# Retention in 64-token chunks from the fifth block on, with its output product split around the next block's states and scores

## The chip, the cores and the metric

One core of a Trainium2 chip runs the kernel. The metric is the time of one execution in microseconds of device time, as the median of several runs. The engines are named as in the profile: PE (TensorE, matrix products; PEld is its weight load), DVE (VectorE), ACT (ScalarE), POOL (GpSimd) and SP (SyncE, which issues most of the transfers). Products go to PSUM; DVE and ACT read them from there.

## What is computed

Two stages follow each other. The first is retention, a causal attention without softmax whose weights decay with distance. The second is a feed-forward layer with the activation h·cos(h).

```python
batch, n_heads, seq, head_dim = (8, 8, 576, 64)
scores = scale * np.matmul(q, k.transpose(0, 1, 3, 2))
gamma = 1.0 - 2.0 ** (-5.0 - np.arange(H, dtype=np.float32))
rel = pos[:, None] - pos[None, :]
Dmat = np.where(rel >= 0, gamma[:, None, None] ** rel[None, :, :], 0.0)
attn_out = np.matmul(scores * Dmat, v)
# 4608 tokens; 8 heads of 64 side by side
x = attn_out.transpose(0, 2, 1, 3).reshape(B * S, H * D)
h = x @ w_in            # 512 -> 2048
out = (h * np.cos(h)) @ w_out   # 2048 -> 512
```

## The kernel before

**Retention in blocks and chunks.** The 4608 tokens are 18 blocks of 256 (`BK`). The decay is put into q and k beforehand (`scaled`, L156: every token's q and k are multiplied by a power of gamma of its position, on POOL for most blocks), so that retention becomes plain causal linear attention. A block is cut into two chunks of 128 tokens. For each chunk and head there are four kinds of matrix products: *scores* (tile `sc`, L282), keys of the chunk against its queries, which DVE multiplies by a 0/1 causal mask on the way to `ret` (L292); *states* (tile `st`, L319), the 64x64 matrix of keys times values of the chunk; DVE adds it to the running sum `s` (L347 copies where a sequence begins, L349 adds), and ACT rounds the sums to `sb` (L359); the chunk's *own output* (tile `ov`, L375), masked scores times values; and the *carried output* (L407), queries times the rounded sum of all chunks before, into the same PSUM tile. ACT then rounds `ov` into the feed-forward input `xT` (L430). Blocks 0 to 3 order their tokens in even/odd pairs (`pair`, `NP_B = 4`) and have products and code paths of their own. A sequence has 576 tokens, so with chunks of 128 some are `mixed`: a sequence ends and another begins in their middle. Those use `mask_cmix`, and `v_odd`, a copy of the values with the first half zero.

Products of 64 contraction rows by 64 output columns use a quarter of the PE array; in the trace four of them, on the four quarters, start within some 10 ns. The score and carried products are such quarters, 128 tokens wide. The state and own products of a 128-token chunk use all 128 contraction rows and half of the columns.

**Feed-forward in rounds.** The feed-forward layer works in nine rounds, n = 0 to 8, of 512 tokens (`W`), two blocks each. In a round, `mm1` (L435) makes h in eight pieces; each piece has a PSUM tile `h` in one of the banks "a", "b" and "m" (each 4 KB for a partition, in the order `abmabmab` for most rounds, so that the eighth piece is in "b"). ACT makes cos(h) as a sine (L457), and DVE multiplies h by it into `gT` (L460). After that comes the second product, by a seven-product scheme (`mm2_seven`, L582): products 1, 2, 6, 4, 7, 5 and 3, in that order, 16 products each, into the small banks "n" (1, 6 and 7 accumulate there, then 3) and "st" (2, 4 and 5, each over the one before). It needs sums of quarters of `gT`, the tiles `gs` (`g_sum`, L487), on DVE and, for one of them, on POOL. ACT copies finished products to `ot` (`copied`, L592), DVE adds others to them (L590), and SP stores the results.

**Who orders the work.** The program is scheduled by hand: each engine runs its instructions in the order in which the code issues them. Between two of the seven products the code calls a *unit* from the table `at`, which does a part of the retention of the blocks for the next round. In rounds 3 to 7 there are two visits in a round: `first_unit` before product 2 and `second_unit` before product 5. A visit issues the states of the next block (into bank "st"), the output of the block before it (bank "m"), and the scores of the next block (its two chunks into banks "a" and "b"). Rounds 1 and 2 have units of their own (`first_scores`, `next_scores`, `last_outputs`; `only_intro`, `mid_unit`, `end_unit`), as the lead of the retention over the feed-forward layer is built up there. DVE operations that need not come at once (the second mask, the adds) are kept in `pend` and issued by the next `flush()`. In a first visit the issue order on DVE is: state sums, the rest of the sums `gs` 5 and 6 (`late_sums`), first mask, the add that frees bank "st" for product 4, second mask. In a second visit it is: state sums, the add that frees bank "n" for product 3, the masks. A step of preparation (POOL scales q and k and rounds v of a later block, SP transposes by DMA and loads another block) hangs on the stores.

Of the kernel before, what the change touches and what calls it, by code (L numbers as in the profile page):

```python
# [8 lines left out]
F32 = mybir.dt.float32  # L9
# [8 lines left out]
def kernel(  # L18
# [34 lines left out]
    MIX = PERK // 2  # L53
    AHEAD = 3
# [28 lines left out]
    mask_c = consts.tile([P, P], F32)  # L83
    mask_cmix = consts.tile([P, P], F32)
# [4 lines left out]
    v_odd = consts.tile([P, H, D], BF16)  # L89
# [5 lines left out]
    class Chunk:  # L95


        def __init__(self, j, k):
            self.j, self.k = j, k
            self.pair = j < NP_B  # L100
            self.rows = slice(k * HP, k * HP + HP) if self.pair else slice(0, P)
            self.t0, self.c0, self.p0 = j * BK + k * P, k * P, k * HP
            first, end = self.t0 % S, (self.t0 + P - 1) % S
            self.mixed = end < first
            self.fresh = first == 0 or self.mixed
            self.carry = 0 if first == 0 else S - first if self.mixed else P
            self.ends = end == S - 1

    chunks = [[Chunk(j, k) for k in range(2)] for j in range(NB)]
# [64 lines left out]
    def round_v(j, runs=(nc.gpsimd.tensor_copy,) * 2):  # L174
# [4 lines left out]
        for c in chunks[j]:  # L179
            if c.mixed and c.pair:  # L180
                nc.scalar.copy(v_mix[HP // 2 : HP], vb[HP // 2 : HP])
                nc.scalar.copy(v_mix[HP:], vb[HP:])
            elif c.mixed:
                nc.gpsimd.tensor_copy(v_odd[HP:], f[HP:, c.k])
# [40 lines left out]
    def q_cols(c, he, hg, n=HP):  # L225

        return tiles["qkT", c.j][he * D : he * D + D, 0, :, hg, c.p0 : c.p0 + n]

    def scores(j, banks):
# [3 lines left out]
        pss = [  # L233
            psum.tile([P, HG, 2, P], F32, tag=t, name="sc")
            if isinstance(t, str)
            else [psum.tile([P, HG, P], F32, tag=u, name="sc") for u in t]
            for t in banks
        ]
        if cs[0].pair:
            order = [(c, y, he, hg) for hg in range(HG) for y in range(2) for he in range(2) for c in cs]  # L240
            mask = mask_mix if any(c.mixed for c in cs) else mask_p
            for c, y, he, hg in order:
# [4 lines left out]
                    rhs=q_cols(c, he, hg),  # L247
# [22 lines left out]
        else:  # L270
            ret = ret.rearrange("p a b r i -> p (a b r i)").rearrange(
                "p (k a b i) -> p k a b i", k=2, a=2, b=HG
            )
            pss = [
                ps.rearrange("p b r i -> p (b r i)").rearrange("p (a b i) -> p a b i", a=2, b=HG)
                for ps in pss
            ]
            for c in cs:
                for hg in range(HG):
                    for i0 in range(0, P, HP):  # L280
                        for he in range(2):
                            nc.tensor.matmul(  # L282
                                pss[c.k][i0 : i0 + HP, he, hg, :],
                                lhsT=kT[he * D : he * D + D, 1, c.k, hg, i0 : i0 + HP],
                                rhs=q_cols(c, he, hg),
                                start=True,
                                stop=True,
                            )

            def masked(k):  # L290
                mask = mask_cmix if cs[k].mixed else mask_c
                nc.vector.tensor_tensor(  # L292
                    out=ret[:, k].rearrange("p a b i -> p (a b) i"),
                    in0=pss[k].rearrange("p a b i -> p (a b) i"),
                    in1=mask.unsqueeze(1).to_broadcast([P, H, P]),
                    op=ALU.mult,
                )
# [4 lines left out]
    def sums_of(j, bank):  # L302
# [3 lines left out]
        ps = psum.tile([P, 2, HG, D], F32, tag=bank, name="st")  # L306
        begun = set()
        for c in need:
            if pair:
                vb = v_mix if any(c.mixed for c in need) else tiles["vb", j]  # L310
                rows = slice(0, P) if c.k == 1 and need[0].k == 0 else c.rows
                parts = [(y, vb[rows, y]) for y in range(2)]
            else:
                rows = c.rows
                parts = [(c.k, v_odd if c.mixed else tiles["vb", j][:, c.k])]
            for hg in range(HG):
                for y, vs in parts:
                    for he in range(2):
# [3 lines left out]
                            rhs=vs[:, head(he, hg), :],  # L322
                            start=he not in begun,
                            stop=y == parts[-1][0],
# [4 lines left out]
        def add():  # L329
            s32 = stp.tile([P, len(need), HG, D], F32, tag="s32", name="s32")  # L330
# [13 lines left out]
            else:  # L344
                for u, c in enumerate(need):
                    if c.fresh:
                        (nc.scalar.copy if j == 4 else nc.vector.tensor_copy)(s32[:, u], ps[:, c.k])  # L347
                    else:
                        nc.vector.tensor_tensor(  # L349
                            out=s32[:, u],  # L350
                            in0=ps[:, c.k],
# [5 lines left out]
            def rounded(run=nc.scalar.copy):  # L357
                sb = stp.tile([P, len(need), HG, D], BF16, tag="sb", name="sb")
                run(sb, s32)  # L359
# [7 lines left out]
    def out_own(j, ps):  # L367
# [4 lines left out]

        def one(c, h, y, rhs):
            part = (h % 2, h // HG)
            nc.tensor.matmul(  # L375
                ps[h % 2 * D : h % 2 * D + D, h // 2, c.c0 : c.c0 + P],
                lhsT=vb[c.rows, y, h, :],
                rhs=rhs,
                start=part not in begun,
                stop=False,  # L380
                skip_group_check=True,
            )
            begun.add(part)

        if chunks[j][0].pair:
            for swap in (1, 0):
                for hg in range(0, HG, 2):
                    for c in chunks[j]:
                        he = c.k ^ swap
                        for y in range(2):  # L390
                            for h in (head(he, hg), head(he, hg + 1)):
                                one(c, h, y, ret[c.rows, he, h % HG, y, :])
                if swap:
                    nc.tensor.drain()
        else:
            for c in chunks[j]:
                for h in range(H):
                    one(c, h, c.k, ret[:, c.k, h // HG, h % HG, :])

    def out_carried(j, ps):  # L400
        cs = [c for c in chunks[j] if c.carry]
        for hg in range(0, HG, 2):
            for c in cs:
                n = c.carry // 2
                for h in [head(he, hg + u) for u in range(2) for he in range(2)]:
                    he = h // HG
                    nc.tensor.matmul(  # L407
                        ps[h % 2 * D : h % 2 * D + D, h // 2, c.c0 : c.c0 + P].rearrange(
                            "p (r i) -> p r i", r=2
                        )[:, :, :n],  # L410
                        lhsT=s_before[c][he * D : he * D + D, h % HG, :],
                        rhs=q_cols(c, he, h % HG, n),
# [11 lines left out]
    def outputs(j, bank, evac=nc.scalar.copy, evac2=None):  # L424
        ps = psum.tile([P, DG, BK], F32, tag=bank, name="ov")
        out_own(j, ps)
        out_carried(j, ps)
        x = x_of(j)
        if evac2 is None:
            evac(x, ps)  # L430
        else:
            evac(x[:, :2], ps[:, :2])
            evac2(x[:, 2:], ps[:, 2:])
# [148 lines left out]
    def mm2_seven(n, at, stored, xs=(1, 2, 6, 4, 7, 5, 3), halfway=None):  # L582
# [9 lines left out]
        def copied(tag, x):  # L592
            t = op.tile([P, 2, N2], F32, tag=tag, name="ot")
            nc.scalar.copy(t, tiles["all", x])  # L594
# [9 lines left out]

        for x in xs:
            if x in at:
                at[x](flush, pend)
            else:
                flush()
# [45 lines left out]
            else:  # L655
                flush()
                for (j, c0, c1), ps in zip(parts, tiles["o", 5]):
# [84 lines left out]
    nc.gpsimd.memset(ones, 1.0)  # L742
    nc.gpsimd.affine_select(
# [315 lines left out]
```

## Time and profile before

| | |
|---|---|
| median of 3 runs | 294.61 us (294.57 to 294.89) |
| span of the profiled execution, first to last instruction | 293.2 us |
| whole time of such an execution, by the runs | 294.6 us, 1.4 us more than the span |
| PE busy | 284.1 us, 97% of the span, 3268 products |
| DVE busy | 215.6 us, 74% |
| ACT busy | 142.9 us, 49% |
| POOL busy | 145.5 us, 50% |
| products of blocks 4 to 17 | scores L282 448, states L319 240, own L375 224; carried L407 256 with the earlier blocks |

Busy times of PE are unions of pipelined products, each of which lasts about 0.2 us from start to end while others start every few nanoseconds; so the distance from start to start says more than a product's own length. A line of the timeline gives the start, the length of the whole group (with the tail of its last product), the engine, the source line and the shape: `64*64 64x128` is a quarter product of 64 rows by 64 columns that streams 128 columns.

### The profile page before, as it was taken

The page shows a single profiled execution, that of the slowest core. Times are in us where ns is not written, and L with a number is a line of the kernel's source. Part 1 is how long each engine was busy: PE and PEld are TensorE (multiplying, and loading weights), DVE is VectorE, ACT ScalarE, POOL GpSimd, SP SyncE. Part 2 cuts the span into 40 slices and gives each one's busy share as a digit, 9 for nine tenths or more (in the row PEclk, how much of TensorE's full clock was granted, in tenths as well). Part 3 has the DMA queues.
Part 4 walks back from the last instruction along what each step waited for, and adds up shares of the span by engine and source line. Part 5 has one row for each costly group of instructions (what it writes and reads, how often), then busy time and mean ns, then how long its engine had stood idle before and what let it go on. Part 6 is the DMA issues. An engine that isn't in the chain of part 4 may idle for free.

```text
span 293.2 us, 7643 instructions
## 1 busy us (share of the span) xinstructions
PE 284.1 (97%) x3268; PEld 194.8 (66%) x3268; DVE 215.6 (74%) x267; ACT 142.9 (49%) x166; POOL 145.5 (50%) x172
## 2 busy tenths in 40 slices
PE   6899999999999999999999999999999999999994
PEld 2568655878864687458845884588458845874583
DVE  4675748558967989699759975997599759835933
ACT  3567437646436533663366335633663356326620
POOL 8641355856586916779354871497248014102400
PEclk9799999999999999999999999999999999999998
DMA  7999999999999999999999999999950630122013
GB/s 197 267 223 215 229 256 201 239 192 164 217 216 197 210 170 229 235 214 209 229 200 203 219 175 222 217 223 223 208 78 21 127 72 0 38 65 45 2 37 107
DMA packets 128930, 49.78 MB, mean 170 GB/s; under 512 B 89344, under 2 KB 128384, under 8 KB 128896
## 3 DMA queue, kind: packets, MB, share of 16 engines
q1 hardware_dynamic: 124144, 44.71, 77.3%
q0 software_dynamic: 4224, 4.19, 8.7%
q8 instruction: 25, 0.41, 0.6%
q10 hardware_dynamic: 528, 0.39, 0.4%
q14 instruction: 9, 0.07, 0.1%
HBM read 36.70 MB, written 9.44 MB: 157 GB/s over the span
## 4 chain that ended last, share of the span: by engine, by line
PE 93%; DVE 2%; DMA 1%; ACT 1%; issue 0%; DVEq 0%; ACTq 0%
PE h L445 42%; PE o L564 34%; PE o L935 5%; PE ov L375 3%; PE st L319 2%; PE sc L282 2%; PE ov L407 2%; DMA fk<-in_k_dram 1%; PE tr L210 1%; DVE ret L262 1%; PE sc L244 1%; DVE qks L167 0%; PE idle L220 0%; DVE gT L460 0%; DVE ret L255 0%
## 5 line engine op out<-in xcount | busy, mean ns | idle before, releaser
L445 PE MATMUL h<-xT,w_in_sb 128*128 128x512 bf16 (+1 forms) x704 | 127.3, 340 | 0.2
L460 DVE TENSOR_TENSOR gT<-h,cosh 128x1024 bf16<-128x1024 f32 x72 | 87.9, 1221 | 37.2 <-ACT cosh L457 37.1
L457 ACT ACTIVATE cosh<-h,half_pi 128x1024 f32<-128x1024 f32 x72 | 80.2, 1114 | 65.5 <-PE h L445 64.3
L445 PEld LDWEIGHTS <-w_in_sb 128*128 128x128 bf16 x704 | 68.4, 98 | 55.3 <-issue 0.6
L503 POOL TENSOR_TENSOR gs<-gT 128x512 bf16<-128x512 bf16 x28 | 36.3, 1298 | 76.9 <-DVE gT L460 76.9
L564 PEld LDWEIGHTS <-gs 128*128 128x128 bf16 x528 | 49.5, 98 | 6.5
L167 POOL TENSOR_TENSOR qks<-fq,gq 128x512 bf16<-128x512 f32 x31 | 33.8, 1110 | 28.2 <-DMA fq<-in_q_dram 23.6
L564 PEld LDWEIGHTS <-gT 128*128 128x128 bf16 x384 | 36.9, 98 | 6.9 <-DVE gT L460 0.5
L594 ACT COPY ot<-o 128x512 f32<-128x512 f32 x33 | 19.3, 586 | 41.2 <-PE o L564 41.2
L590 DVE TENSOR_TENSOR ot<-ot,o 128x512 f32<-128x512 f32 x35 | 23.2, 680 | 11.4 <-ACT ot L594 7.9
L167 POOL TENSOR_TENSOR qks<-fk,gkc 128x512 bf16<-128x512 f32 x28 | 31.0, 1122 | 1.1 <-DMA fk<-in_k_dram 1.0
L564 PE MATMUL o<-w_out_sb,gT 128*128 128x256 bf16 x256 | 30.8, 273 | 0.0
L564 PE MATMUL o<-w_out_sb,gs 128*128 128x256 bf16 (+1 forms) x264 | 30.6, 269 | 0.0
L564 PE MATMUL o<-ws,gs 128*128 128x256 bf16 (+1 forms) x264 | 30.5, 270 | 0.0
L292 DVE TENSOR_TENSOR ret<-sc,mask_c 128x1024 bf16<-128x1024 f32 x25 | 29.7, 1214 | 0.1
L178 POOL CAST vb<-fv 128x512 bf16<-128x512 f32 x31 | 19.3, 637 | 6.1 <-DMA fv<-in_v_dram 5.8
L430 ACT CAST xT<-ov 128x1024 bf16<-128x1024 f32 x16 | 16.2, 1013 | 10.2 <-PE ov L407 10.2
L503 DVE TENSOR_TENSOR gs<-gT 128x512 bf16<-128x512 bf16 (+1 forms) x25 | 16.5, 661 | 0.4
L349 DVE TENSOR_TENSOR s<-st,s 128x256 f32<-128x256 f32 x18 | 7.6, 422 | 10.6 <-PE st L319 10.3
L564 PE MATMUL o<-ws,gT 128*128 128x256 bf16 x128 | 15.3, 273 | 0.0
L935 PE MATMUL o<-w_out_sb,gT 128*128 128x512 bf16 x64 | 15.0, 380 | 0.0
L503 DVE TENSOR_TENSOR gs<-gs,gT 128x1024 bf16<-128x1024 bf16 x16 | 14.7, 920 | 0.3
(81 smaller groups left out, 198.5 us busy)
## 6 DMA issues: line engine op xcount, KB each, us to landing
out_dram<-ot SPq DMA_DIRECT2D x68, 128.0 KB, 2.6
fk<-in_k_dram SPq DMA_DIRECT2D x25, 256.0 KB, 5.7
fv<-in_v_dram SPq DMA_DIRECT2D x25, 256.0 KB, 5.5
fq<-in_q_dram SPq DMA_DIRECT2D x12, 512.0 KB, 5.5
w_in_sb<-in_moe_w_in_dram POOLq DMA_DIRECT2D x4, 512.0 KB, 8.1
w_out_sb<-in_moe_w_out_dram POOLq DMA_DIRECT2D x4, 512.0 KB, 9.8
fk<-in_k_dram SPq DMA_DIRECT2D x3, 512.0 KB, 5.4
fv<-in_v_dram SPq DMA_DIRECT2D x3, 512.0 KB, 7.0
```

Of the source, the lines that this page charges most:

```text
L167: return eng.tensor_tensor(out=dst.rearrange("p b a d -> p a b d"), in0=src.rearrange("p (a b) d -> p a b d", a=2), in1=by.rearrange("p (a ...
L178: runs[y](vb[:, y], f[:, :, y, :] if j < NP_B else f[:, y])
L292: nc.vector.tensor_tensor(out=ret[:, k].rearrange("p a b i -> p (a b) i"), in0=pss[k].rearrange("p a b i -> p (a b) i"), in1=mask.unsqueez ...
L430: evac(x, ps)
L445: nc.tensor.matmul(ps[:, j, :], lhsT=w_in_sb[:, dg, (et + j) * P : (et + j + 1) * P], rhs=xT[:, dg, c0 : c0 + w], start=(dg == 0), stop=(d ...
L457: nc.scalar.activation(cosh, ps, ACTF.Sin, bias=half_pi, scale=1.0)
L460: nc.vector.tensor_mul(gT[:, et : et + m, c0 : c0 + w], ps, cosh)
L503: i = eng.tensor_tensor(out=tiles["gs", n, x][:, e : e + step], in0=a[:, e : e + step], in1=b[:, e : e + step], op=op_,)
L564: nc.tensor.matmul(dst[i], lhsT=lhs[:, e, j * P : (j + 1) * P], rhs=rhs[:, e, c0:c1], start=(fresh and e == 0 and (i == 0 or len(parts) > 2)),
L590: return lambda: nc.vector.tensor_tensor(out=out_, in0=in0, in1=in1, op=ALU.add)
L594: nc.scalar.copy(t, tiles["all", x])
L935: nc.tensor.matmul(pss[t], lhsT=gT[:, e, t * P : (t + 1) * P], rhs=w_out_sb[:, e, :], start=(e == 0), stop=(e == ET - 1),)
```

## The change

From block 4 on a chunk has 64 tokens, so a block has four. A chunk's keys sit in one half of the partitions (`half`), and chunks 0 and 1 form the first 128 tokens, 2 and 3 the second (`y`). All four kinds of products are now quarters with 64 streamed columns, 32 of each kind for a block (fewer carried ones, and fewer states, where a sequence begins or ends); 576 is a multiple of 64, so no such chunk is mixed, and `v_odd` and `mask_cmix` go. The scores of a block fill one bank instead of two; each mask instruction has 128x512 elements instead of 128x1024. The state sums are up to four instructions for a block in place of up to two. They are written to one constant buffer `s_all`, and ACT rounds up to 1024 columns.

The own output is made in two passes (`swap`): in each pass the two row halves write to different PSUM banks, and in the second they change places. Between the passes `visit` puts the states and scores of the next block, and a copy of one column on ACT (`flag`): it waits for the last product of pass one, and the first product of pass two waits for it. Where nothing lies between (blocks 5 and 17), a drain of PE separates the passes. The states of a visit go to bank "b" instead of "st", the scores to "a". The ACT copies of finished products are kept in `held` and issued behind that flag copy.

```diff
 class Chunk:
+            size = P if self.pair else HP
+            self.half = k if self.pair else k % 2
+            self.y = None if self.pair else k // 2
+            self.rows = slice(self.half * HP, self.half * HP + HP)
...
+    chunks = [[Chunk(j, k) for k in range(2 if j < NP_B else 4)] for j in range(NB)]
...
 def scores(j, banks):     # blocks from 4 on
+            ps = psum.tile([P, 2, HG, 2, HP], F32, tag=banks[0], name="sc")
+            for hg in range(HG):
+                for c in cs:
+                    for he in range(2):
+                        nc.tensor.matmul(
+                            ps[c.rows, he, hg, c.y, :],
+                            lhsT=kT[he * D : he * D + D, 1, c.y, hg, c.rows],
+                            rhs=q_cols(c, he, hg, c.n),
...
 def sums_of(j, bank):     # blocks from 4 on
+            ps = psum.tile([P, 2, 2, HG, D], F32, tag=bank, name="st")
+            for hg in range(HG):
+                for c in need:
+                    for he in range(2):
+                        nc.tensor.matmul(
+                            ps[he * D : he * D + D, c.half, c.y, hg, :],
+                            lhsT=tiles["qks", j][c.rows, 1, c.y, hg, he, :],
+                            rhs=tiles["vb", j][c.rows, c.y, head(he, hg), :],
...
         def add():
-            s32 = stp.tile([P, len(need), HG, D], F32, tag="s32", name="s32")
+            s32 = s_all[:, : len(need)]
...
 def out_own(j, ps, guard=None):
+        for swap in (1, 0):
+            for hg in range(0, HG, 2):
+                for c, y in order:
+                    he = c.half ^ swap
+                    for h in (head(he, hg), head(he, hg + 1)):
...
+            if swap and guard is None:
+                nc.tensor.drain()
+            elif swap:
+                gate = nc.scalar.copy(flag[:, 1:], flag[:, :1])
+                after(gate, i)
+                while held:
+                    held.pop(0)()
+                guard()
...
         def copied(tag, x):
             t = op.tile([P, 2, N2], F32, tag=tag, name="ot")
-            nc.scalar.copy(t, tiles["all", x])
+            held.append(lambda ps=tiles["all", x]: nc.scalar.copy(t, ps))
             return t
...
-    def intro(j, sc_banks, st_bank, put_off=None, then=None):
-        add = sums_of(j, st_bank)
-        rounded = add()
-        if then:
-            then()
-        masks = scores(j, sc_banks)
+    def visit(j, sc_bank, st_bank, put_off=None, then=None, out_of=None):
+        masks, rounded = [], []
+        def middle():
+            rounded.append(sums_of(j, st_bank)())
+            if then:
+                then()
+            masks.extend(scores(j, [sc_bank]))
+        if out_of:
+            outputs(*out_of, middle)
+        else:
+            middle()
         masks[0]()
...
         def first_unit(flush, pend):
             def then():
                 late_sums(n, (5, 6))
                 flush()
-                outputs(a, "m")
-            intro(b, "ab", "st", pend, then)
+            visit(b, "a", "b", pend, then, (a, "m"))
...
         def second_unit(flush, pend):
+            if b + 1 < NB:
+                visit(b + 1, "a", "b", pend, flush, (b, "m"))
```

`mid_unit`, `end_unit`, `only_intro` and `next_scores` change in the same way.

## The prediction

> **What bounds the kernel now.** I read the page first. TensorE (PE) is busy 97% of the span at full granted clock, and the chain that ended last is PE for 93%, nearly all of it the two feed-forward products.
>
> ```profile
> PE 284.1 (97%) x3268; PEld 194.8 (66%) x3268; DVE 215.6 (74%) x267; ACT 142.9 (49%) x166; POOL 145.5 (50%) x172
> ...
> PE 93%; DVE 2%; DMA 1%; ACT 1%; issue 0%; DVEq 0%; ACTq 0%
> ```
>
> So an edit is worth what it takes from PE's stream, unless another engine is just behind. The timeline of PE over the two visits of round 5 (512 tokens; lines 951 and 959) shows both kinds of visit. Columns: start, length of the group, instructions.
>
> ```profile
> 188.94 1.91 PE L564 MATMUL o<-w_out_sb,gT 128*128 128x256 bf16 x16
> 190.78 0.32 PE L319 MATMUL st<-vb,qks 128*64 128x64 bf16 x8
> 190.93 0.62 PE L375 MATMUL ov<-ret,vb 128*64 128x128 bf16 x16
> 191.48 0.42 PE L407 MATMUL ov<-qkT,sb 64*64 64x128 bf16 x16
> 191.73 0.62 PE L282 MATMUL sc<-qkT 64*64 64x128 bf16 x32
> 192.28 1.92 PE L564 MATMUL o<-w_out_sb,gT 128*128 128x256 bf16 x16
> 194.03 1.91 PE L564 MATMUL o<-ws,gs 128*128 128x256 bf16 x16
> 195.80 1.91 PE L564 MATMUL o<-ws,gT 128*128 128x256 bf16 x16
> ...
> 199.38 0.44 PE L319 MATMUL st<-vb,qks 128*64 128x64 bf16 x16
> ```
>
> The first visit lasts from 190.78 to 192.28, 1.50 us. Then I read VectorE (DVE) and GpSimd (POOL) over the same stretch, to see who is just behind.
>
> ```profile
> 190.29 1.22 DVE L460 TENSOR_TENSOR gT<-h,cosh 128x1024 bf16<-128x1024 f32 x1
> 191.44 0.41 DVE L347 COPY s<-st 128x256 f32<-128x256 f32 x1
> 191.77 0.80 DVE L503 TENSOR_TENSOR gs<-gT 128x512 bf16<-128x512 bf16 x1
> 192.60 1.41 DVE L503 TENSOR_TENSOR gs<-gs,gT 128x1024 bf16<-128x1024 bf16 x1
> 193.94 1.21 DVE L292 TENSOR_TENSOR ret<-sc,mask_c 128x1024 bf16<-128x1024 f32 x1
> 195.07 0.67 DVE L590 TENSOR_TENSOR ot<-ot,o 128x512 f32<-128x512 f32 x1
> ...
> 191.25 2.22 POOL L167 TENSOR_TENSOR qks<-fq,gq 128x512 bf16<-128x512 f32 x2
> 193.43 2.49 POOL L167 TENSOR_TENSOR qks<-fk,gkc 128x512 bf16<-128x512 f32 x2
> ```
>
> DVE runs without a gap, and its L590 add ends at 195.74, 0.05 before product 4 starts at 195.80: that product overwrites the bank "st" that the add reads. In round 3 PE already waits 0.05 there. So **in the first visit DVE is as critical as PE**. The second visit has slack: DVE idles 2.29 us before it. The `gs` sums also take turns with POOL: 0.42 and 0.69 us in round 7, where POOL is idle, but 1.41 for the second in rounds 3 to 6, each time ending 0.585 after a POOL instruction does.
>
> **The change on PE.** Start to start, four quarter products of 128 columns take 0.056 us, a pair of half-array state products of 64 columns 0.0315; a change of tile shape costs 0.09. No sustained run of 64-column quarters is in the trace; in round 4 two groups of four, alternating with two of 128 columns, fill 0.20 us, which fits 0.03. Bounds: 0.028 (the closest two there) and 0.056 (no gain from the shorter columns); I take 0.0315, the row of the same width and length of run. A visit now has four groups of 8 such fours (own output, states, scores, carried), one shape throughout: 0.15 (pass one, with 0.02 for the first four) + 0.25 + 0.25 + 0.13 + 0.25 + 0.10 to go back = 1.13 us, or 1.06 with a fresh chunk. Before: 1.49 to 1.73. PE alone would save 0.36 to 0.6 a visit, 6 us over all.
>
> The gate of pass two: the last product of pass one ends 0.19 after its start, ACT starts 0.05 later (as after L407), a copy of one column takes about 0.19 (the 128x1 sine 0.20), the way back 0.05: 0.48 us against 0.50 of states and scores. Hidden, with ACT idle there; without cover it costs what it lacks, 0.19 in round 1, where only scores lie between. Blocks 5 and 17 get a drain instead, 0.27 us (L394: 0.32 between products instead of 0.056), which eats their saving.
>
> **What the change adds behind PE.** (1) States move from bank "st" to "b". At the first visit of rounds 3 to 7, "b" still holds the last `h`, until the L460 multiply ends. The order of the changed kernel has a VectorE wait at the first state product there, and none in the second visit. In round 5: 190.29 + 1.22 = 191.52, PE resumes at 191.57. Pass one ended at 190.93: **a stall of 0.64 us**, with scores and pass two queued behind it. Product 2 starts 0.98 later (0.25 + 0.25 + 0.13 + 0.25 + 0.10), at 192.55; it was 192.28.
>
> (2) State sums: three or four 128x256 instructions where one or two were, each 0.46 after the one it depends on, 0.34 if free. They sit on DVE ahead of the `gs` sums, mask and add. The halved masks give back 0.53 each (1.13 between starts to 0.60, as the 128x512 mask at L255).
>
> Round 5, first visit. States reach DVE 0.48 after PE resumes, 192.05; three instructions, 0.34 + 0.45 + 0.34, bring the first `gs` to 193.18. POOL turns over at 191.25, 192.25, then 193.25 (1.00 each when unshared). The first `gs` gets in at 193.25, POOL's next, delayed 0.18, runs to 194.43, the second `gs` ends at 195.02 (before: 194.02). Mask from 194.94, add 195.54 to 196.21, product 4 at 196.27: 0.47 later than 195.80. (PE by itself would be there at 192.55 + 2 x 1.755 = 196.06, and the second half of product 6, which reads the second `gs`, comes due at 195.2, in time.) The same steps:
>
> - round 3: sums ready 134.95, past POOL's turn at 134.56, so the one at 135.56; product 4 at 138.58, before 137.10: +1.47
> - round 4: ready 163.87, turn 163.82 missed by 0.05: +1.36 (caught: +0.36)
> - round 6: ready 222.44, turn 222.51: +0.36 (missed: +1.36)
> - round 7: no POOL; PE is last, 250.21 + 0.05 + 0.98 + 3.51 = 254.75, before 254.47: +0.28
>
> Rounds 5 and 6 catch their turn by only 0.07; a miss costs 1.0 each.
>
> Second visits, rounds 3 to 6: product 3 overwrites bank "n", which an add behind the four sums reads. States reach DVE 0.61 after the visit's start; 3 x 0.46 + 0.34 + 0.68 + 0.05 later product 3 may start: 3.06 us. PE alone would be there at 1.06 + 1.75 = 2.81. Before: 3.26 to 3.33. So 0.2 to 0.27 is kept of 0.45 to 0.5, 0.93 in all. Round 7's second visit: 0.04 lost to the drain.
>
> Round 2: the last visit needs both masks of the one before (four sums, then masks), ready 3.67 after that one's start, at 112.5, where the states start now; its length falls from 1.73 to 1.13: -0.6. Round 1: gains of 0.3 are lost to the same gs and mask chain: 0, give or take 0.3.
>
> Edits with one answer: the three `v_odd` copies (0.95 each on POOL) end behind casts nobody waits for, 0; ACT's longer roundings (0.2 to 0.4) lie in its 51% idle, 0; the held ACT copies run 0.6 later, still a microsecond before their readers, 0, or up to 0.1 in round 2; setup on POOL is about 1 us shorter beside loads, 0. Queue order on SP stays, its stores wait up to 1.5 us longer, loads are a round ahead.
>
> Sum: 1.47 + 1.36 + 0.47 + 0.36 + 0.28 - 0.93 + 0.04 - 0.6 = +2.45; with the wake-up of a two-semaphore wait (0.14 in round 1 instead of 0.05) about +2.6. Against the span of 293.2: 295.8; 1.4 us lie around it to the median of 294.61: **297.2 us**.
>
> [...] Row: in round 3, 48 quarter products start within 0.70 us, 0.015 each, with products ready in the queue. [...]
>
> **Rivals.**
> 1. Faster: DVE is not last. If `gs` and POOL did not take turns and sums overlapped, only the bank-"b" stall (+0.15 to 0.3 a round) would stay, and second visits and rounds 1 and 2 keep their full 0.5: -2 to -3, about 292. It decides once the first `gs` is ready before POOL's earlier turn, 0.7 us sooner than I have it. Four of four rounds end the second `gs` 0.585 after a POOL instruction, against it. Chance 0.08.
> 2. PE can't start quarters fast enough once more than 48 follow each other: 0.056 a four (the worst bound) makes a visit 1.9 us: +0.35 instead of -0.23 in second visits, +0.8 in first ones and round 2: +9, about 303. Against: the four of a group start 3 ns apart, and no gap in a run of 48 says that the supply ran out. Chance 0.06. [...]
> 3. All POOL turns caught in rounds 4 to 6: +1.4, 296; all missed: +4.6, 299.2. These belong to the forecast.
> 4. The edits cancel: turns caught and round 1 gaining 0.5 to 1: about 294.6. Chance 0.06.
>
> Forecast 0.80. The range, 295.2 to 299.4, takes in rival 3. A measurement here can tell some 0.2% (0.6 us). Slower 0.86, same 0.06, faster 0.08.
>
> **What would show it.** Right: in the changed profile a PE gap of about 0.6 us before the first state product of rounds 3 to 7, ended by the DVE multiply that writes `gT`; state, score, own groups at 0.25 us; product 4 starting right after the add; DVE groups of sums 0.46 apart. Wrong: no gap there, fours at 0.05, or the second `gs` ending with no relation to POOL.

## The result, and the profile after

The changed kernel takes 304.85 us (median of 4 runs, 303.63 to 305.98), the kernel before 294.75 us beside it on the same chip (4 runs, 294.57 to 295.07): 1.034 times as long, 95% interval 1.030 to 1.037. The forecast of 297.2 us (295.2 to 299.4) had the sign and a quarter of the size. The profiled execution has a span of 304.3 us (its time 305.98); before it was 293.2 us.

From the page of the changed kernel: engines, the granted TensorE clock in 40 slices, the instruction queue, and the chain that ended last.

```profile
PE 284.9 (94%) x3892; PEld 192.9 (63%) x3892; DVE 212.2 (70%) x292; ACT 149.8 (49%) x178; POOL 142.0 (47%) x167
...
PEclk9999999999999997997999999999999999999999
...
q8 instruction: 30, 0.49, 0.7%
...
PE 64%; DVE 16%; DMA 7%; issue 5%; POOL 4%; ACT 3%; SPq 1%; DVEq 0%; POOLq 0%; ACTq 0%
```

PE is busy for as long as before (284.9 us and 284.1), but its share falls from 97% to 94%. DVE now holds 16% of the chain (2% before), which fits the forecast. Two things are not in the forecast. "issue" has 5% (0% before); its two longest pieces, 2.18 and 2.21 us, lie in rounds 2 and 3. And two slices there have a granted clock of 7 tenths. The timeline of PE at the last visit of round 2 and the first visit of round 3 (start, length of the group, instructions, idle time before it and its releaser):

```profile
112.15 0.32 PE L400 MATMUL ov<-ret,vb 64*64 64x64 bf16 x16
112.30 0.23 PE L427 MATMUL ov<-qkT,sb 64*64 64x64 bf16 x6
114.70 0.41 PE L427 MATMUL ov<-qkT,sb 64*64 64x64 bf16 x26 [2.18 <-issue]
115.04 3.28 PE L577 MATMUL o<-w_out_sb,gs 128*128 128x256 bf16 x16
...
136.22 0.83 PE L577 MATMUL o<-w_out_sb,gT 128*128 128x256 bf16 x6
139.26 2.31 PE L577 MATMUL o<-w_out_sb,gT 128*128 128x256 bf16 x10 [2.21 <-issue]
```

PE stops in the middle of the carried products, after 6 of 32, and in the middle of product 2, after 6 of 16. "issue" says that the profile shows nothing that it waits for. Start to start the two gaps are 2.37 and 2.49 us, 2.34 and 2.38 more than the pace. Behind each the clock falls to half. Busy time in stretches of 3.41 us, with the granted clock third from last:

```profile
111.99:115.40 3.41, 1.23 (x88) 1.04 (x76) 3.20 (x8) 0.35 (x2) 2.69 (x3) 1.00 1.01 180
115.40:118.81 3.41, 3.41 (x17) 2.21 (x15) 0.94 (x2) 1.50 (x2) 2.33 (x4) 0.50 1.03 254
135.87:139.28 3.41, 1.20 (x54) 0.83 (x42) 3.27 (x6) 1.96 (x2) 3.41 (x4) 1.00 0.97 163
139.29:142.70 3.41, 3.41 (x17) 2.43 (x18) 1.70 (x4) 0.00 (x0) 1.09 (x2) 0.50 0.90 163
```

Each gap leaves PE 1.2 us of work in a stretch of 3.41 us, and the next 3.41 us run at half clock, which costs half of that, 1.7 us, more. So a gap of 2.3 us costs 4.

Round 5 shows what the forecast was about (compare its lines of before; the PE lines come first, then DVE, then POOL):

```profile
198.64 0.32 PE L400 MATMUL ov<-ret,vb 64*64 64x64 bf16 x16
199.52 0.38 PE L315 MATMUL st<-vb,qks 64*64 64x64 bf16 x21 [0.56 <-DVE gT L473]
...
200.59 1.92 PE L577 MATMUL o<-w_out_sb,gT 128*128 128x256 bf16 x16
202.35 1.04 PE L577 MATMUL o<-ws,gs 128*128 128x256 bf16 x8
203.92 1.05 PE L577 MATMUL o<-ws,gs 128*128 128x256 bf16 x8 [0.54 <-DVE gs L516]
205.11 1.91 PE L577 MATMUL o<-ws,gT 128*128 128x256 bf16 x16
```

```profile
198.14 1.23 DVE L473 TENSOR_TENSOR gT<-h,cosh 128x1024 bf16<-128x1024 f32 x1
200.01 0.42 DVE L364 TENSOR_TENSOR s_all<-st,s_all 128x256 f32<-128x256 f32 x1 [0.64 <-PE st L315]
...
200.80 0.42 DVE L364 TENSOR_TENSOR s_all<-st,s_all 128x256 f32<-128x256 f32 x1
201.14 1.28 DVE L516 TENSOR_TENSOR gs<-gT 128x512 bf16<-128x512 bf16 x1
202.45 1.42 DVE L516 TENSOR_TENSOR gs<-gs,gT 128x1024 bf16<-128x1024 bf16 x1
```

```profile
199.10 2.04 POOL L172 TENSOR_TENSOR qks<-fq,gq 128x512 bf16<-128x512 f32 x2
201.10 2.22 POOL L172 TENSOR_TENSOR qks<-fk,gkc 128x512 bf16<-128x512 f32 x2
```

The states wait for the multiply that frees bank "b". The DVE sums come behind, and the first `gs` comes up at 201.14, just after POOL has started its next instruction at 201.10. It lasts 1.28 us instead of 0.80, so product 6 waits in its middle and product 4 starts 8.31 us after product 1 instead of 6.86.

Where 11.0 of the 11.1 us between the two profiled executions went, from the start of product 1 of one round to that of the next (before round 2: from the span's start):

| stretch | foreseen | measured | difference |
|---|---|---|---|
| until product 1 of round 2 | 0 | -0.98 | -1.0 |
| round 2 | -0.6 | +3.44 | +4.0 |
| round 3 | +1.2 | +4.16 | +2.9 |
| round 4 | +1.1 | +1.24 | +0.1 |
| round 5 | +0.2 | +1.40 | +1.2 |
| round 6 | +0.1 | +1.32 | +1.2 |
| round 7 | +0.3 | +0.46 | +0.1 |

("Foreseen" is a first visit's term and, in rounds 3 to 6, a quarter of -0.93 for the second.) The two gaps with their half clock fill rounds 2 and 3; the missed turns fill rounds 5 and 6.

### The profile page after: what moved, and what is told of

The parts are those of the page before. It is cut to its first block, busy times and chain, and to the rows that moved or that the text cites. A ratio compares the mean times of both kernels' runs of the same rounds, so it can differ in the third digit from the quotient of the medians.

```text
span 304.3 us, 8932 instructions
## 1 busy us (share of the span) xinstructions
PE 284.9 (94%) x3892; PEld 192.9 (63%) x3892; DVE 212.2 (70%) x292; ACT 149.8 (49%) x178; POOL 142.0 (47%) x167
## 4 chain that ended last, share of the span: by engine, by line
PE 64%; DVE 16%; DMA 7%; issue 5%; POOL 4%; ACT 3%; SPq 1%; DVEq 0%; POOLq 0%; ACTq 0%
PE h L458 28%; PE o L577 25%; DVE gT L473 9%; PE o L969 5%; DVE gs L516 3%; DMA w_in_sb<-in_moe_w_in_dram 3%; POOL qks L172 3%; DMA fk<-in_k_dram 2%; ACT cosh L470 2%; PE ov L400 2%; DMA qkT<-qks 2%; DVE s_all L364 1%; PE st L315 1%; DVE ot L603 1%; PE ov L427 1%
## 5 line engine op out<-in xcount | busy, mean ns | idle before, releaser
L473 DVE TENSOR_TENSOR gT<-h,cosh 128x1024 bf16<-128x1024 f32 x72 | 88.0, 1222 | 38.1 <-ACT cosh L470 38.0
L577 PE MATMUL o<-w_out_sb,gT 128*128 128x256 bf16 x256 | 31.7, 278 | 2.2 <-issue 2.2
L577 PE MATMUL o<-ws,gs 128*128 128x256 bf16 (+1 forms) x264 | 31.7, 273 | 1.6 <-DVE gs L516 1.6
L577 PE MATMUL o<-w_out_sb,gs 128*128 128x256 bf16 (+1 forms) x264 | 32.0, 277 | 0.3
L364 DVE TENSOR_TENSOR s_all<-st,s_all 128x256 f32<-128x256 f32 x43 | 18.2, 424 | 19.0 <-PE st L315 17.3
L172 POOL TENSOR_TENSOR qks<-fk,gkc 128x512 bf16<-128x512 f32 x28 | 29.8, 1083 | 0.7 <-DMA fk<-in_k_dram 0.7
L183 POOL CAST vb<-fv 128x512 bf16<-128x512 f32 x31 | 20.7, 689 | 4.4 <-DMA fv<-in_v_dram 4.4
L374 ACT CAST sb<-s_all 128x768 bf16<-128x768 f32 (+2 forms) x18 | 15.6, 868 | 10.5 <-DVE s_all L360 3.8
L295 DVE TENSOR_TENSOR ret<-sc,mask_c 128x512 bf16<-128x512 f32 x28 | 18.4, 681 | 0.0
L516 DVE TENSOR_TENSOR gs<-gT 128x512 bf16<-128x512 bf16 (+1 forms) x25 | 17.2, 689 | 0.4
```

The lines of the kernel that those rows point to most:

```text
L172: return eng.tensor_tensor(out=dst.rearrange("p b a d -> p a b d"), in0=src.rearrange("p (a b) d -> p a b d", a=2), in1=by.rearrange("p (a ...
L183: runs[y](vb[:, y], f[:, :, y, :] if j < NP_B else f[:, y])
L295: nc.vector.tensor_tensor(out=ret[:, he].rearrange("p b y i -> p (b y) i"), in0=ps[:, he].rearrange("p b y i -> p (b y) i"), in1=mask_c.un ...
L364: nc.vector.tensor_tensor(out=s32[:, u], in0=ps[:, c.half, c.y], in1=s32[:, u - 1] if u else tiles["run"], op=ALU.add,)
L473: nc.vector.tensor_mul(gT[:, et : et + m, c0 : c0 + w], ps, cosh)
L516: i = eng.tensor_tensor(out=tiles["gs", n, x][:, e : e + step], in0=a[:, e : e + step], in1=b[:, e : e + step], op=op_,)
```

## The experiments

**A theory for the gaps.** PE's instructions come in packets on queue q8: the page has 30 packets and 0.49 MB, 16 KB each. Take a packet as a page of 256 instructions (the burst below bears this out), a product and its weight load being one each. Then the 3892 products and their loads are 30.4 pages, the two gaps stand behind 1626 and 1882 products, so 512 instructions apart, and they end 1.28 and 1.22 us after a q8 packet has landed. A full visit now has 256 such instructions in 1.1 us; before it had 144 or 160 in 1.5 to 1.7 us. *Supply theory:* PE has used up a page of instructions before the next is there. *Data theory:* PE waits at these places for data, by a wait that the trace does not show.

**Pages moved: 174 and 126 instructions ahead.** If idle products are put at the very start, where PE only waits for the first loads, every page boundary falls on another instruction and nothing else changes. The author's estimate by the supply theory was 298 us with 174 (297 to 300), both gaps gone or under 1.2 us and the half clock with them. The "stretch of 3.7 us" expected with 126 is likewise an estimate, of the time that PE has work on a page; in the trace of the changed kernel the 256 instructions that end at 82.4 us take 3.39 us from start to start.

```diff
-    warm(11, "n")
+    warm(10, "n")
+    quarters(88, "m")     # 88 idle 64x64x64 products; 64 in the other
```

> The changed kernel with one idle product of 512 columns at the very start replaced by 88 idle quarter products, in time in which TensorE only waits for the first loads; every later instruction of TensorE is the same but has 174 more ahead of it. [...] Data theory (TensorE waits at these two places for something that the trace does not show, states rounded by ACT or a transfer): both gaps stay at the same product, 304 to 306 us.

> The same with 64 quarter products, 126 more instructions ahead of everything. Supply theory: the gap of round 3 goes; that of round 2 stays but lies some 126 instructions earlier in the same visit, among its states or scores instead of its carried products, 2 to 3 us long; a new gap of 1.5 to 3 us comes in round 1, in its last visit about 82.4 us, where there is none now (stretch of 3.7 us); 301 to 306 us. Data theory: the gaps of rounds 2 and 3 stay at the same products and none comes in round 1.

Measured: 302.45 us with 174 (4 runs, 300.12 to 304.67) and 303.27 us with 126 (301.94 to 304.58), profiled in executions of 300.12 us, the fastest of the four, and of 303.35 us, in the middle of its four; spans 298.4 and 301.6. With 174 both gaps and both half clocks are gone: of the 5.9 us by which the span is shorter, round 2 gives 3.7 and round 3 gives 2.8. A gap appears in round 4, where there was none:

```profile
163.76 1.70 PE L586 MATMUL o<-w_out_sb,gT 128*128 128x256 bf16 x14
166.58 0.38 PE L586 MATMUL o<-w_out_sb,gT 128*128 128x256 bf16 x2 [1.12 <-issue]
```

With 126 the gap of round 3 goes too, that of round 2 moves forward into the states and shrinks to 0.42 us (2 to 3 expected), and the new one foreseen in round 1 is there, with 3.41 us of half clock behind it (from 85.67):

```profile
82.90 0.43 PE L436 MATMUL ov<-qkT,sb 64*64 64x64 bf16 x31
84.90 0.19 PE L436 MATMUL ov<-qkT,sb 64*64 64x64 bf16 x1 [1.57 <-issue]
```

So the gaps follow the page boundaries and not the data; the data theory falls. The gap of round 1 was forecast in its place; that of round 4 with 174 was not, and the lengths came out only roughly. The median with 174 lies above the estimate. Its four executions are 4.5 us apart; that other boundaries come out short, and not equally so each time, would explain both, but one execution of a kernel was profiled, so that is not shown.

**The supply by itself.**

```diff
+            if x == 6 and n in (5, 8):
+                quarters(512, "b")      # in the kernel before
```

> The kernel before with 512 idle quarter products of 64 columns (1024 instructions) put ahead of product 6 in round 5, with transfers under way, and in round 8, with hardly any; they wait for no data. Supply theory: the first 100 to 250 products start 0.008 us apart, then come gaps, one for each 256 instructions, 3 to 7 us from one to the next in round 5 (the burst takes 14 to 26 us), shorter in round 8 (8 to 16 us). Data theory, or a start rate as the sum had it: 512 x 0.0079 = 4.1 us in both. If products of 64 columns cannot start that close for long, no gaps but an even pace above 0.01 us.

Measured: span 328.5 us. PE's timeline in round 5 (transfer engines busy until about 209 us) and round 8 (from 305.6 us on transfer engines 1 to 2% busy):

```profile
196.33 2.72 PE L227 MATMUL idle<-zeros 64*64 64x64 bf16 x215 [2.75 <-DVE ret L301]
200.98 1.92 PE L227 MATMUL idle<-zeros 64*64 64x64 bf16 x128 [1.93 <-issue]
207.73 1.92 PE L227 MATMUL idle<-zeros 64*64 64x64 bf16 x128 [4.82 <-issue]
211.73 0.80 PE L227 MATMUL idle<-zeros 64*64 64x64 bf16 x41 [2.08 <-issue]
```

```profile
300.81 2.44 PE L227 MATMUL idle<-zeros 64*64 64x64 bf16 x247
305.61 1.47 PE L227 MATMUL idle<-zeros 64*64 64x64 bf16 x128 [2.37 <-issue]
309.34 1.92 PE L227 MATMUL idle<-zeros 64*64 64x64 bf16 x128 [2.26 <-issue]
313.34 0.37 PE L227 MATMUL idle<-zeros 64*64 64x64 bf16 x9 [2.08 <-issue]
```

This settles it. The first 247 products of round 8 start 0.009 us apart (0.008 in the sum). Then PE stops after every 128 products, that is 256 instructions. From page to page it takes 3.73 and 4.00 us with nothing else on the transfer engines, 6.75 us beside the kernel's loads and transposes, and 4.00 us in the next stretch, where these run out (29% busy). The transfers of that stretch of round 8 show the two pages that PE waited for, and nothing else (from the DMA view, 305.7 to 313.3 us):

```profile
DMA packets 2, 0.03 MB, mean 4 GB/s; under 512 B 0, under 2 KB 0, under 8 KB 0
## 3 DMA queue, kind: packets, MB, share of 16 engines
q8 instruction: 2, 0.03, 1.7%
```

The packets agree: 16 KB each, and one for every 256 instructions. At 0.009 us a product PE is through a page in about 1.2 us, and in the burst the next one came no sooner than 3.73 us after the one before. How far ahead of its use a page is asked for is not shown. Both gaps of the changed kernel stand 180 instructions past a multiple of 256. Counted from the product just ahead of such a place to the product just ahead of the next, so without the gap, the shortest page of the kernel before lasts 6.9 us. With the change the page that ends at the gap of round 2 lasts 3.8, that of round 3 lasts 2.6, and four without a gap lie between 2.6 and 4.0. So this count tells that pages became short, not which of them falls short.

**Banks changed over.** This and what follows has the 174 ahead, so it is compared with the kernel that has these alone (span 298.4).

```diff
-            visit(b, "a", "b", pend, then, (a, "m"))
+            visit(b, "b", "a", pend, then, (a, "m"))   # states in "a", scores in "b"
```

> The kernel with 174 more instructions ahead, and in the first visit of rounds 3 to 7 the banks of states and scores changed over: states in "a", scores in "b", so that the scores and not the states wait for the last multiply of the feed-forward part. Against the kernel with 174 more alone: if the state stall is as the prediction has it (bank "b" free when the multiply ends), the wait of 0.72 us before the states goes and one of about 0.47 us comes before the scores; the state sums on VectorE start right after the multiply, some 0.45 us earlier, which by the prediction's times catches POOL's turn in rounds 4 to 6: about 1.0 us less in each, 3 us in all (0.3 to 0.4 a round if turns are still missed, 1.2 in all). If the first visit is bound by something else, for example the number of products in it, no change.

Measured: 300.32 us (296.4 to 300.8), span 294.7, 3.7 us less (both profiled executions are the fastest of their four; the medians differ by 2.1 us, less than either kernel's spread). The scores wait instead of the states, by 0.37 to 0.50 us. The DVE sums start as the multiply ends, and the `gs` sums get in a turn earlier (round 5):

```profile
191.00 1.23 DVE L482 TENSOR_TENSOR gT<-h,cosh 128x1024 bf16<-128x1024 f32 x1
192.14 0.41 DVE L373 TENSOR_TENSOR s_all<-st,s_all 128x256 f32<-128x256 f32 x1
...
193.26 1.02 DVE L525 TENSOR_TENSOR gs<-gT 128x512 bf16<-128x512 bf16 x1
194.31 1.42 DVE L525 TENSOR_TENSOR gs<-gs,gT 128x1024 bf16<-128x1024 bf16 x1
```

Product 1 to product 4 is 7.32 to 7.33 us in rounds 4 to 6 instead of 8.33 (8.57 in round 4, with its gap): 1.0 us each, one turn of POOL, as expected.

**`gs` sums ahead of the state sums.**

```diff
-            def then():
+            def first():                    # called before the sums of the states
                 late_sums(n, (5, 6))
                 flush()
```

> The kernel with 174 more instructions ahead; in the first visit of rounds 3 to 7 VectorE does the last parts of the sums gs 5 and 6 before the state sums, not behind them. By the turns of POOL: the first of them is ready when the last multiply ends, gets in at the turn before, the second ends about 1.0 us earlier than now, and the second half of product 6 does not wait (now 0.7 us); state sums, mask and add come behind, so that the start of product 4 follows the add: product 1 to product 4 7.6 to 7.8 us instead of 8.3 in rounds 3, 5 and 6. If the second sum ends 0.585 after a POOL instruction only by chance, product 6 still waits and nothing is gained.

Measured: one execution, span 300.2. Product 6 does not wait any more, and product 1 to product 4 is 7.44 us in rounds 5 and 6 (8.02 in round 3; round 4 lost 1.03 to a page boundary). The order on DVE, not the stall of the states alone, made product 6 late. The gain of 0.9 us a round did not reach the span, since gaps of 1.04 and 1.63 us and a half clock came in round 2.

**The add ahead of the state sums in second visits.**

```diff
-                visit(b + 1, "a", "b", pend, flush, (b, "m"))
+                flush()
+                visit(b + 1, "a", "b", pend, None, (b, "m"))
```

> The kernel with 174 more instructions ahead; in the second visit of rounds 3 to 6 the add that product 3 waits for (bank "n") goes ahead of the four state sums on VectorE. If that chain is what holds product 3, as the sum had it, the visit's start to product 3 falls from about 3.2 us to 2.85 us (what TensorE needs by itself, 1.10 + 1.75) in each of four rounds, 1.4 us in all; if the visit itself is longer than the sum had it, it stays.

Measured: one execution, span 298.8. From product 5 to product 3 it takes 1.75 us, the length of a product, instead of 2.01: the wait of 0.26 us is gone in rounds 3 to 6, a little less than the 0.35 expected, since the visit by itself takes 1.19 us and not 1.06 to 1.13. The 1 us won in all is again less than the page boundaries add in round 2 (1.17 and 0.95 us).

**A drain instead of the gate.**

```diff
-            outputs(*out_of, middle)
+            middle()
+            outputs(*out_of)
```

> The kernel with 174 more instructions ahead, with a drain between the two passes of the output in every visit, states and scores ahead of pass one, no gate by ACT. If the gate is hidden behind states and scores as the sum had it, each visit becomes 0.2 to 0.27 us longer where TensorE is last (second visits, round 2), and in first visits the stall before the states stays at 0.72 + 0.15 with pass one behind it: 1 to 3 us more in all. If the gate costs something in every visit, the drain makes visits shorter.

Measured: one execution, span 309.8, 11.4 us more, not 1 to 3. The visit itself is 0.26 us longer where the lines can be compared (product 7 to product 5 of rounds 4 and 5: 3.28 and 3.29 us instead of 3.02 and 3.03). That is nearly all of the 0.27 forecast for a drain, so the gate costs little there: in the second visits of the changed kernel the scores take 0.29 to 0.30 us up to pass two instead of 0.25 (0.38 in round 6). But without the gate the held copies on ACT come behind the roundings of `ov` and of the state sums, product 3 waits 0.9 us for its bank in rounds 3 to 6 (0.3 with the gate), and a gap of 3.0 us with a half clock came in round 2. As a test of the gate alone it is spoilt by that.

**All of it together.** Banks changed over, the scores of the first visit at its end, DVE in the order `gs`, add, state sums, masks, and the add first in second visits.

```diff
+        if late:
+            adds = []
+            outputs(*out_of, lambda: adds.append(sums_of(j, st_bank)))
+            then()
+            masks = scores(j, [sc_bank])
+            put_off += [lambda: adds[0]()(), *masks]
+            return
```

> Together: 174 more instructions ahead; first visit of rounds 3 to 6 with states in bank "a" and scores in "b" put at the end of the visit, behind the carried products, so that nothing waits for the last multiply; gs sums first on VectorE, then the add that product 4 waits for, then state sums and masks; the add ahead of the state sums in second visits. By the sum: product 1 to product 4 3 x 1.755 + 1.13 + 0.1 to 0.4 = 6.5 to 6.8 us instead of 8.3, second visits 0.35 less: 8 us less than the span of 298.4 of the kernel with 174 more, 290.5, and 292 us with gaps of supply of 0 to 2 us that fall elsewhere: 290.5 to 295, so probably a little below the kernel before. If the supply of instructions is the bound and not VectorE's chain, these microseconds come back as gaps: 297 or more.

Measured: 296.81 us (12 runs, 294.8 to 298.81) beside 295.15 us for the kernel before (17 runs); ratio 1.0065, interval 1.0041 to 1.0089. That is above the 290.5 to 295 us expected. DVE's part is solved: product 1 to product 4 takes 6.74 to 6.76 us in rounds 5 to 7, less than the 6.83 to 6.96 of before. The stops at page boundaries, 0.90, 1.50 and 0.97 us in rounds 2 and 4 of the profiled execution, add up to more than the 1.1 us by which its span (294.3) exceeds that of before.

**Visits of round 2 farther apart, at three alignments.**

```diff
-            at = {6: only_intro, 5: mid_unit, 3: end_unit}
+            at = {6: only_intro, 7: mid_unit, 3: end_unit}
```

> The reordered kernel (with 174 more instructions ahead), and in round 2 the middle visit before product 7 instead of product 5, so that two products and not one lie between it and the last visit. Supply theory: in the reordered kernel the gaps at page boundaries are 0.90 and 1.50 us in round 2, 0.78 in round 3, 0.97 in round 4; with the visits farther apart those of round 2 shrink to 0 to 1 us together, and the wait of 0.85 us for the masks before the last visit goes: 1.5 to 3 us less, span 291.3 to 292.8, time 293 to 295.5. If the gaps of round 2 come from something else in that round (the transposing transfer, the loads), they stay and only 0.85 us is gained.

> The same with nothing put ahead, so page boundaries as in the changed kernel. [...] Data theory: same places as with 174 ahead.

> The same with 128 quarter products (254 instructions, two short of a page) put ahead: the page boundaries lie at almost the same instructions as with nothing ahead, one page later in the count. Supply theory: gaps at the same products as with nothing ahead (to within two instructions), of like length, 293 to 298 us; times of this and of the one with nothing ahead agree within 1 us. If only the number of instructions ahead or the time at the start mattered, not the place in the page, it would look like the one with 174.

Measured, with the kernel before at 294.92 us (20 runs, 294.04 to 297.7): 295.39 us with 174 ahead (ratio 1.001, interval 0.998 to 1.005), 297.92 us with none (1.009), 297.10 us with 254 (1.007), each within the range expected (for none the author's estimate was 293 to 298 us). The last two are two instructions short of a whole page apart, and their gaps stand at the same products (none ahead first, then 254, product 2 of round 3):

```profile
134.65 0.83 PE L577 MATMUL o<-w_out_sb,gT 128*128 128x256 bf16 x6
138.07 1.13 PE L577 MATMUL o<-w_out_sb,gT 128*128 128x256 bf16 x7 [2.59 <-issue]
```

```profile
133.95 0.94 PE L586 MATMUL o<-w_out_sb,gT 128*128 128x256 bf16 x7
136.69 1.14 PE L586 MATMUL o<-w_out_sb,gT 128*128 128x256 bf16 x9 [1.80 <-issue]
```

The same holds for round 2 (carried products, after 6 and after 7 of 32). With 174 ahead there is no gap in product 2 of round 3. So the place within the page decides, not the number of instructions ahead. The other traces agree. The changed kernel and its nine versions without the added drains have 23 stops of PE of over 0.2 us behind the first 55 us that the profile puts down to "issue"; counted in products and weight loads, each stands 178 or 180 instructions past a multiple of 256. Spreading the visits removed the wait for the masks. With 174 ahead the profiled execution still has 0.51 and 2.59 us at the boundaries of round 2, where at most 1 us was expected, and 2.92 us in round 4. But it is the slowest of the ten (300.56 us, mean granted clock 0.986); the others took 294.12 to 297.9 at 0.996 to 1.000, so it is not typical of them. In that one, two products between the last visits instead of one did not make the page long enough. No version has a median below that of the kernel before.

## Why the prediction was right or wrong

**Right: the first visit.** The stall before the states is 0.72 to 0.75 us, counted from where the next product was due (0.64 and the wake-up foreseen), ended by the L473 multiply. Quarters of 64 columns ran at 0.25 us for eight fours. Round 4 came out at +1.36 us from product 1 to product 4, the price of its missed turn; round 7 at +0.46 (+0.28 foreseen). The start rate of quarters, on which the sum rests, holds: 247 products in a row at 9 ns. The row of 48 starts in the prediction has them in 0.65 us, 0.014 each, and not in 0.70.

**Wrong, rounds 2 and 3: the bound put on a dense run of products.** The step that failed is in rival 2: "no gap in a run of 48 says that the supply ran out." A run of 48 products is 96 instructions, and a page has 256, so no run of the kernel before could have shown it. The supply was named, but as an even pace of 0.056 us a four (303 us, chance 0.06), and it was set aside on evidence about an even pace; the sum has no term for it. That 303 lies near the measured 304.85 is chance: the fours kept their 0.03. In its place the runs show stops at page boundaries, with a half clock behind them: 4.0 us over the forecast in round 2 and 2.9 in round 3, where the gap also hid DVE's delay. They make 7.0 of the 8.6 us between the forecast change and the measured one. The trace of before had the material for the question: 25 packets of 16 KB on the instruction queue, and 256 instructions of a visit in 1.1 us.

**Wrong, rounds 5 and 6: the turns.** The text has "Rounds 5 and 6 catch their turn by only 0.07", and later adds 0.15 us in all for a wait on two semaphores, but to the sum alone. Here PE resumed 0.15 us after the multiply and not 0.05, which by itself is more than the 0.07 in hand, and the first sum came 0.49 us after that. Both turns were missed: 1.0 us more each up to product 4, and 1.2 with the second visits. The price of a miss was right, and banks changed over won it back.

**Wrong in size: second visits.** They gave back 0.05 to 0.12 us each instead of 0.2 to 0.27: product 3 started 3.19 to 3.28 us after the visit did, not 3.06. That the DVE chain held it was right.

**Missing: the start.** The first product of round 1's feed-forward part is 0.57 us earlier, and round 1 itself gained 0.41 us; both were put at nothing. No run was made to find out why.

## What to carry to other kernels

Count the instructions of an engine as well as its time: a change that makes products smaller and closer can let PE use up a page of 256 instructions before the next one is there. In the burst pages came 3.73 to 6.75 us apart, and in the changed kernel the two that end at a gap last 3.8 and 2.6 us. A mid-product gap that the profile puts down to "issue" is to be compared with the landing of the instruction packets; if idle instructions put at the start, less than a page of them, move it, it is supply. Where a step is caught or missed by less than the error of the sum, take the miss into the forecast.

## What the runs showed of the hardware

- PE's instructions arrive in 16 KB packets (30 for the 30.4 pages of the changed kernel). The stops shown here end 1.2 to 1.7 us after such a packet has landed. With idle transfer engines a page came every 3.73 to 4.00 us in the burst, so PE could not keep up more than 256 instructions, 128 products of 64x64x64, in 3.73 us there.
- A gap shorter than 3.41 us was enough to halve the clock. The stretches of 3.41 us before the half clock had 1.20 and 1.23 us of busy PE, and the half clock lasts 3.41 us; the two of the changed kernel start 23.89 us apart, seven times that. Gaps of 2.4 us were enough there, each of them inside the 3.41 us ahead of the half clock, and with 126 ahead one of 1.76 us. Busy time alone does not decide in these runs. After 1.61 us, in 16 full-array products (254 ahead, visits apart, a gap of 2.07 us), the clock stayed full; after 1.85 us in 126 products, nearly all quarters (`gs` sums first), and after 1.74 us in 72 products, 64 of them quarters (126 ahead), it was halved. What else decides is not shown. First the version with 254 ahead, then the one with the `gs` sums first:

```profile
134.60:138.01 3.41, 1.61 (x16) 1.29 (x15) 1.50 (x2) 0.23 (x1) 3.41 (x4) 1.00 0.88 228
...
111.91:115.32 3.41, 1.85 (x126) 1.44 (x124) 2.17 (x5) 1.01 (x3) 3.17 (x4) 1.00 0.66 136
115.32:118.73 3.41, 2.96 (x15) 1.94 (x13) 2.95 (x6) 1.67 (x2) 1.47 (x2) 0.50 0.93 239
```

- The spread of executions differed: 2.4 us in 4 runs of the changed kernel, 4.5 and 2.6 in 4 with the pages moved. The kernel before had 0.5 us in 4 runs, 2.0 in 7, 1.9 in 17 and 3.7 in 20, so how much of it comes with the change is not shown.

Open is what sets the time that a page takes beside other transfers (6.75 us in the one page measured so), and at which instruction it is asked for. In round 2 of the two kernels with none and 254 ahead, the middle visit also waited 1.3 to 1.5 us for the transposing transfer. A visit inside the first feed-forward product, where 16 instructions fill 1.7 us, was not tried.
